# A fused attention and two-MLP kernel: the last 64 features of q and k in another matmul form, x loaded in two transfers, and another order of the program

## Chip, core and metric

One core of one Trainium2 chip runs the whole kernel. The metric is device time in microseconds (us), the median of several executions, lower is better. Engines are called as the profile does: PE (TensorE, matmuls), PEld (its weight loads, which overlap the matmuls), DVE (VectorE), ACT (ScalarE), POOL (GpSimd), SP (SyncE, whose queue issues the transfers).

## The reference

One sequence of 2048 tokens, 448 features, bf16. Attention has 16 heads of 28 features and a dilated local window: token s looks at the 8 tokens s, s-2, ..., s-14. Around it stand layer norms, a residual, and a block with two small MLPs. Cut to what matters:

```python
qkv = layernorm(x) @ wqkv                       # 2048 x 448 by 448 x 1344
logits[s, w] = q[s] . k[s - 2 w] / sqrt(28)     # w = 0..7, per head, -1e9 where s - 2 w < 0
o = sum over w of softmax(logits)[s, w] * v[s - 2 w]
h = x + o @ wo

b = layernorm(h)
g = gelu(layernorm(b) @ w1)                     # 448 x 448
g = four quarters of the features, shifted by +1, -1, +2, -2 tokens
x1 = b + g @ w2                                 # 448 x 448
h2 = gelu(layernorm(x1) @ w3) @ w4              # 448 x 1792, 1792 x 448
out = h + x1 + h2
```

## The kernel before

**Tiling.** Tokens go in 4 stages t of 512 (tiles of 128 tokens) through attention and w1, and then in 5 units u of 2, 4, 4, 4 and 2 tiles through w2, w3 and w4. The phases of a stage are N1 (layer norm of x), A1 (transpose the normalised tokens and project them on q and k), V (project on v), A2 (products of q with eight shifted copies of k on DVE, summed over a head's features by matmuls with a 0/1 matrix `zc`, then the softmax, which ends in `pb` and its transposed copy `pt`), A3 (`pt` spread by a mask into `bd_r` on DVE, then matmuls with the windowed values `vw`, then the product with wo, called O), B1 (two layer norms in one, a transpose, then w1 with gelu, called M). The phases of a unit are B2 (w2, residual), T (norm and transpose), W3 (w3, gelu) and B3 (w4, output). Stages and units overlap freely.

**Matmuls.** The contraction over 448 features lies in four chunks, whose upper and lower 64 partitions are separate matmuls, so that one with its weights in partitions 0 to 63 and one in 64 to 127 run side by side. `duo` (L459) makes two output tiles at once that way, in two operations: a first half (8 matmuls) and a second half (6), where tile and partition half change places. The second half carries an explicit wait for the end of the first (`op.sdeps.update(turned)`), because the two halves write the same two PSUM banks from opposite halves of the array. Other work may stand between the two.

**The last 64 features of q and of k** do not fill a block of 128 outputs. Before, A1 (L692 to L706) makes them as 64 x 64 quarters: four matmuls of 64 partitions by 64 outputs by 256 tokens form a set (two partition halves, two output halves), 28 matmuls a stage in two operations of 16 and 12, the second of which waits for the first in the same way. `X` is q, `Y` is k; the 512 tokens are split so that the even 64s of each 128 lie in the upper and the odd 64s in the lower 64 partitions of the output. ACT then evicts them: q as one 128 x 256 copy into `qT`, k as 128 x 4 x 64 into `kr`, which is four blocks of 80 columns (16 columns of earlier tokens ahead of 64 new ones), and the 16 earlier columns of each block in three small copies (L711 to L716).

**What sets the order of the work.** Every operation is recorded first, with its dependences. `ORDER` (L20) is a permutation of the operations' numbers, and each engine runs its own in that order; `OTHER` (L52) lists operations that go to their other engine (an eviction that is by default on ACT goes to DVE, a norm from ACT to DVE, one softmax product from DVE to POOL). All are emitted by one loop at L1010, so nearly every row of the profile has that line, and rows are told apart by names and shapes. SP issues all transfers in program order. `arrange` (L193) makes a DMA transpose wait for the landing of every transfer that stands ahead of it since the last such transpose, and later transfers wait for the transpose. Tokens of t = 0 and 1 are transposed by PE, those of t = 2 and 3 by a DMA transpose (`TURN`, first letters t and d).

**The start.** x is loaded as tile 0, tile 1 and tiles 2 and 3, then wqkv in two parts, then more x. `warm` (L647) puts 11 matmuls of 128 x 512 on a constant matrix ahead of everything on PE; `FILL` may put more of them behind the transposes of each of the first four tiles, and has none before. In A1 of t = 0 the matmuls go by pieces of 256 tokens.

## Time and profile before

| | |
|---|---|
| median of 3 runs | 188.77 us (188.72 to 190.16) |
| profiled execution, from first to last instruction | 186.4 us |
| PE busy, matmuls | 180.3 us, 97% of the span |
| PEld, DVE, ACT, POOL busy | 94.0, 127.0, 122.1, 24.0 us |
| bytes read from and written to memory | 8.14 and 1.84 MB |

The time of the profiled execution itself is given by its span alone: 186.4 us, which is 2.37 us below the median of the runs; that difference lies outside the first and last instruction. A busy share of 97% on PE says that little can be gained on other engines unless PE waits for them, and where it does has to be read by stages, since DVE and ACT are busy 68% and 65% of the whole span but not evenly.

A row of the timeline or of a group gives the start and the length in us, the engine, the line, the operation, out<-in by name, partitions x elements, the count, and in brackets how long the engine had idled and what ended that. On PE, "64*64" is partitions of the weights by outputs.

### The profile page before, as it was taken

What the parts mean: (1) busy time and instruction counts of PE and PEld (TensorE: products, weight loads), DVE (VectorE), ACT (ScalarE), POOL (GpSimd) and SP (SyncE); (2) the same over time, 40 slices, a digit from 0 to 9 for tenths busy, and PEclk for the clock granted to TensorE, in tenths of its full rate; (3) what the DMA queues carried; (4) which work ended last, traced back from release to release, by engine and by line L of the source; (5) the groups of instructions that cost most, each with busy time, mean ns of one, the idle gap of its engine ahead of it and who ended that gap; (6) DMA issues with size and microseconds to landing.
All of it is one profiled execution on the core that took longest, in us unless ns stands there. A gap on an engine that the chain in (4) does not pass through costs nothing.

```text
span 186.4 us, 5772 instructions
## 1 busy us (share of the span) xinstructions
PE 180.3 (97%) x2496; PEld 94.0 (50%) x2496; DVE 127.0 (68%) x225; ACT 122.1 (65%) x289; POOL 24.0 (13%) x59
## 2 busy tenths in 40 slices
PE   6899998999999999999999999999999999999994
PEld 2474333445544565765455544554445544555663
DVE  6799999999999999999476587614087274000403
ACT  3549999898999999957959489503833004730340
POOL 4320000000000000425300000170002805000000
PEclk9999999999999999999999999999999999999999
DMA  5999025865515667914360201491111602300121
GB/s 134 356 282 182 16 51 130 198 216 71 144 38 110 115 216 165 307 53 45 73 116 10 58 8 26 88 141 54 29 40 41 116 0 52 106 0 4 49 98 49
DMA packets 33633, 18.59 MB, mean 100 GB/s; under 512 B 21208, under 2 KB 33096, under 8 KB 33608
## 3 DMA queue, kind: packets, MB, share of 16 engines
q1 hardware_dynamic: 33608, 18.23, 41.5%
q8 instruction: 19, 0.31, 0.6%
q14 instruction: 6, 0.05, 0.1%
HBM read 8.14 MB, written 1.84 MB: 54 GB/s over the span
## 4 chain that ended last, share of the span: by engine, by line
PE 79%; DVE 14%; ACT 4%; DMA 1%; issue 0%; SPq 0%
PE ps L1010 79%; DVE qk_r L1010 9%; DVE st L1010 1%; ACT lntm L1010 1%; DMA xin<-in_A_x_dram 1%; DVE lntm L1010 1%; ACT L1010 1%; DVE mx L1010 1%; DVE xin L1010 1%; ACT arena L1010 1%; ACT h3T L1010 1%; DVE pb L1010 0%; DVE ls L1010 0%; DVE mv L1010 0%; ACT rs_x L1010 0%
## 5 line engine op out<-in xcount | busy, mean ns | idle before, releaser
L1010 PE MATMUL ps<-actT,arena 64*128 64x512 bf16 (+2 forms) x812 | 69.8, 326 | 0.9 <-DMA actT<-lntm 0.5
L1010 ACT ACTIVATE h3T<-ps 128x512 bf16<-128x512 f32 (+1 forms) x70 | 30.9, 517 | 38.5 <-PE ps L1010 38.4
L1010 PEld LDWEIGHTS ps<-actT,arena 64*128 64x128 bf16 (+1 forms) x812 | 35.4, 96 | 31.9 <-PE ps L1010 1.9
L1010 PE MATMUL ps<-arena,h3T 64*128 64x448 bf16 (+3 forms) x434 | 44.9, 343 | 0.2
L1010 ACT ACTIVATE arena<-ps 128x512 bf16<-128x512 f32 (+6 forms) x66 | 30.7, 508 | 8.5 <-PE ps L1010 8.1
L1010 PEld LDWEIGHTS ps<-arena,h3T 64*128 64x128 bf16 (+1 forms) x434 | 22.6, 94 | 20.0 <-ACT h3T L1010 0.6
L1010 DVE TENSOR_TENSOR qk_r<-arena 128x4096 bf16<-128x4096 bf16 (+1 forms) x16 | 31.9, 2013 | 0.1
L1010 DVE SCALAR_TENSOR_TENSOR qk_r<-ps,mrs,arena 128x448 bf16<-128x448 f32 (+2 forms) x17 | 10.4, 651 | 30.9 <-PE ps L1010 30.9
L1010 POOL TENSOR_TENSOR arena<-arena,xin 128x448 f32<-128x448 f32 x16 | 16.1, 1035 | 77.9 <-ACT lntm L1010 65.5
L1010 DVE TENSOR_TENSOR bd_r<-arena,bmask 80x2048 bf16<-80x2048 bf16 x16 | 19.0, 1214 | 1.7 <-PE ps L1010 1.7
L1010 DVE SCALAR_TENSOR_TENSOR arena<-xin,rs_y,ps 128x448 f32<-128x448 bf16 x16 | 10.3, 671 | 11.0 <-PE ps L1010 11.0
L1010 PE MATMUL ps<-wo_s,actT 64*128 64x448 bf16 x128 | 14.5, 350 | 0.1
L1010 PE MATMUL ps<-actT,w_s 64*112 64x512 bf16 x112 | 13.4, 379 | 0.0
L1010 PE MATMUL ps<-w_s,arena 64*128 64x448 bf16 x83 | 12.8, 349 | 0.1
L1010 PE MATMUL ps<-arena,actT 64*128 64x448 bf16 x112 | 12.3, 351 | 0.2
L1010 ACT ACTIVATE actT<-ps 128x512 bf16<-128x512 f32 (+2 forms) x19 | 11.7, 639 | 1.1 <-PE ps L1010 1.0
L1010 ACT ACTIVATE lntm<-xin,nm 128x448 bf16<-128x448 bf16 x16 | 10.6, 672 | 1.1 <-DVE nm L1010 1.1
L1010 DVE BATCH_NORM_STATS2 st<-xin 128x6 f32<-128x448 bf16 x16 | 9.2, 614 | 1.0 <-DMA xin<-in_A_x_dram 0.9
L1010 PEld LDWEIGHTS ps<-actT,w_s 64*112 64x112 bf16 x112 | 7.2, 126 | 4.4 <-ACT arena L1010 0.3
L1010 ACT ACTIVATE rs_x<-mv,epsilon 128x4 f32<-128x4 f32 (+2 forms) x16 | 4.6, 298 | 6.4 <-DVE mv L1010 6.3
L1010 PEld LDWEIGHTS ps<-w_s,arena 64*128 64x128 bf16 x83 | 5.5, 95 | 6.1 <-PE ps L1010 0.5
L1010 ACT ACTIVATE vt<-ps 128x448 bf16<-128x448 f32 x16 | 8.3, 546 | 0.5 <-PE ps L1010 0.5
(73 smaller groups left out, 161.6 us busy)
## 6 DMA issues: line engine op xcount, KB each, us to landing
arena<-in_B_w_dram SPq DMA_DIRECT2D x2, 896.0 KB, 5.9
out_dram<-qk_r SPq DMA_DIRECT2D x15, 112.0 KB, 1.8
arena<-in_B_w_dram SPq DMA_DIRECT2D x2, 784.0 KB, 7.3
vw<-vt SPq DMA_DIRECT2D x4, 320.0 KB, 4.3
vw<-vt SPq DMA_DIRECT2D x4, 256.0 KB, 4.1
arena<-in_A_wqkv_dram SPq DMA_DIRECT2D x2, 448.0 KB, 4.7
xin<-in_A_x_dram SPq DMA_DIRECT2D x2, 448.0 KB, 7.5
xin<-in_A_x_dram SPq DMA_DIRECT2D x3, 224.0 KB, 5.5
```

Of the source, the lines that this page charges most:

```text
L1010: inst = getattr(eng, meth)(**kw)
```

## The change

1. **The last 64 features of q and k become one block of 128 outputs.** POOL copies the 64 weight columns of q and the 64 of k side by side into a new tile `wl` (128 x 4 x 128), as the last operation of the setup (`setup_last`). A1 then makes a `duo` with `wl` as weights: `half(0)` is the first 256 tokens of the stage and `half(1)` the last 256, q in the upper and k in the lower 64 outputs; 8 and 6 matmuls of 64 partitions by 128 outputs by 256 tokens.
2. **Their evictions.** Each half gives two copies of 64 x 256 (q and k), and `kr` becomes one run of 16 + 256 columns with two small copies of 64 x 16 for the earlier tokens (one at t = 3). What lies in which partition half changes with it: now the halves are tokens 0 to 255 and 256 to 511, so the addressing in A2 (`lo`), in the turn of `pb`, in `pt` and in the mask product is permuted; shapes and counts stay the same there.
3. **The loads of x**: tile 0, then tiles 1 to 3 in one transfer, and the two parts of wqkv right behind.
4. **The start on PE**: `WARM` goes from 11 to 8, and `FILL` from none to one matmul each behind the transposes of tile 0 and of tile 1.
5. **A new `ORDER` and `OTHER`.** Of the operations that may go to either engine, those that change: two norms of B1 at t = 0 are on DVE instead of one; the softmax product of t = 3 goes from DVE to POOL; all four evictions of A3 at t = 3 are on DVE instead of three; the one of the first transposes that DVE evicted, and one norm of T at u = 0, go to ACT.

PE at the start. `ps<-ident 128x512` is a warm or fill matmul, `ps<-ident,lntm` a transpose, `ps<-actT,arena 64x256` the quarters and `ps<-actT,wl` the new form (the shape is that of the output). Before:

```order
L1010 MATMUL ps<-ident 128x512 x11
L1010 MATMUL ps<-ident,lntm 128x128 x16
L1010 MATMUL ps<-actT,arena 128x256 x66
L1010 MATMUL ps<-actT,arena 64x256 x16
L1010 MATMUL ps<-actT,arena 128x256 x6
L1010 MATMUL ps<-actT,arena 64x256 x12
```

PE at the start, with the change:

```order
L1007 MATMUL ps<-ident 128x512 x8
L1007 MATMUL ps<-ident,lntm 128x128 x4
L1007 MATMUL ps<-ident 128x512
L1007 MATMUL ps<-ident,lntm 128x128 x4
L1007 MATMUL ps<-ident 128x512
L1007 MATMUL ps<-ident,lntm 128x128 x8
L1007 MATMUL ps<-actT,arena 128x256 x64
L1007 MATMUL ps<-actT,wl 128x256 x8
L1007 MATMUL ps<-actT,arena 128x256 x8
L1007 MATMUL ps<-actT,wl 128x256 x6
```

Three warm matmuls are gone and two stand between the transposes; the 28 quarters are 14 matmuls, and in both orders something stands between their two operations at t = 0.

PE around the last group of t = 3 (`wo_s` is the product with wo, `qk_r,zc` the sums of A2, `arena,actT` the projection on v, `w_s` w1). Before:

```order
L1010 MATMUL ps<-qk_r,zc 32x32x8x2 x16
L1010 MATMUL ps<-arena,actT 128x448 x28
L1010 MATMUL ps<-qk_r,zc 32x32x8x2 x12
L1010 MATMUL ps<-actT,arena 128x512 x28
L1010 MATMUL ps<-actT,arena 64x256 x28
L1010 MATMUL ps<-actT,w_s 112x512 x28
```

With the change:

```order
L1007 MATMUL ps<-actT,wl 128x256 x8
L1007 MATMUL ps<-wo_s,actT 128x448 x8
L1007 MATMUL ps<-xin,ident 128x448 x2
L1007 MATMUL ps<-wo_s,actT 128x448 x8
L1007 MATMUL ps<-xin,ident 128x448 x2
L1007 MATMUL ps<-wo_s,actT 128x448 x8
L1007 MATMUL ps<-xin,ident 128x448 x2
L1007 MATMUL ps<-actT,wl 128x256 x6
L1007 MATMUL ps<-qk_r,zc 32x32x8x2 x24
```

The 28 quarters stood in one piece, so the second operation came directly behind the first; the new group's two halves have the products with wo between them. So they have at t = 0 and 2; at t = 1 the second half is directly behind the first.

SP around its first DMA transpose (`arena<-in_B_w_dram 128x2x1792` is half of w3; `vw<-vt` are the copies that build the windowed values). Before:

```order
L1010 DMA w_s<-in_B_w_dram 128x2x448 x2
L1010 DMA w_s<-in_B_w_dram 112x4x448
L1010 DMA_TRANSPOSE actT<-lntm 128x16x128
L1010 DMA vw<-vt 80x4x512
L1010 DMA vw<-vt 16x3x512
L1010 DMA vw<-vt 64x4x512
L1010 DMA vw<-vt 16x512
L1010 DMA vw<-vt 64x4x512
L1010 DMA vw<-vt 16x3x512
L1010 DMA vw<-vt 80x4x512
L1010 DMA arena<-in_B_w_dram 128x2x1792
```

With the change:

```order
L1007 DMA w_s<-in_B_w_dram 128x2x448 x2
L1007 DMA w_s<-in_B_w_dram 112x4x448
L1007 DMA arena<-in_B_w_dram 128x2x1792
L1007 DMA_TRANSPOSE actT<-lntm 128x16x128
L1007 DMA vw<-vt 80x4x512
L1007 DMA vw<-vt 64x4x512
L1007 DMA vw<-vt 16x3x512
L1007 DMA vw<-vt 64x4x512
L1007 DMA vw<-vt 16x3x512
L1007 DMA vw<-vt 16x512
L1007 DMA vw<-vt 80x4x512
```

The first half of w3 has moved from behind the seven copies to ahead of the transpose, which now waits for its landing.

The diff, cut to its core (of the two tables only the short one):

```diff
 OTHER = """
-92 182 483 489 492 495 546 552
+184 185 483 486 489 492 495 498 555
 """
-FILL = (0, 0, 0, 0)
-WARM = 11
+FILL = (1, 1, 0, 0)
+WARM = 8
...
+        wl = sb("wl", [128, 4, 128], BF16)
...
-        kr = [arv(A_KV + t * KVB + 3 * KVW, 128, 4 * KW).rearrange("p (j n) -> p j n", j=4) for t in range(NST)]
+        kr = [arv(A_KV + t * KVB + 3 * KVW, 128, PADK + 256) for t in range(NST)]
...
-        for i in range(2):
-            load_x(i, 1)
-        load_x(2, 2)
+        load_x(0, 1)
+        load_x(1, 3)
+        load_rows("wqk", wqkv_s[:, :, 0:2 * D], A_wqkv, 0, 2 * D)
         act(zs[:, 0, 0:1], epsilon[:, 0:1], ACT.Exp)
-        load_rows("wqk", wqkv_s[:, :, 0:2 * D], A_wqkv, 0, 2 * D)
...
+        def setup_last():
+            pool("tensor_copy", out=wl[:].rearrange("p c (g n) -> p c g n", g=2),
+                 in_=wqkv_s[:, :, D - 64:3 * D - 64].rearrange("p c (g n) -> p c g n", g=2)[:, :, :, 0:64])
...
-            X, Y = _Tile(P_bank), _Tile(P_bank)
-            both = ((X, D - 64, ((0, 1, 2, 3), (0, 2, 3))), (Y, 2 * D - 64, ((0, 1, 3), (0, 1, 2, 3))))
...
-            copy(qT[:, 3, now:now + 256], X(lambda v: v[:, 0:256]))
-            copy(kr[t][:, :, PADK:], Y(lambda v: v[:, 0:256].rearrange("p (j n) -> p j n", j=4)), False)
-            copy(kr[t][64:128, :, 0:PADK], last(0, 0, 4), False)
-            copy(kr[t][0:64, 1:4, 0:PADK], last(0, 1, 3), False)
+            ends = []
+
+            def half(h):
+                b = _Tile(P_bank)
+                ends.append(b)
+                return sums(lambda lo, n: b(lambda v: v[:, 0:256].rearrange("p (i n) -> p i n", i=2)),
+                            lambda c, part: wl[part, c, :],
+                            lambda c, part, lo, n: rows(a, c, 2 * h, 2, part), h == 0)
+
+            duo(half(0), half(1), ((0, 256),))
+            for h, b in enumerate(ends):
+                copy(qT[64 * h:64 * h + 64, 3, now:now + 256], b(lambda v: v[0:64, 0:256]))
+                copy(kr[t][64 * h:64 * h + 64, PADK:], b(lambda v: v[64:128, 0:256]), False)
+            copy(kr[t][64:128, 0:PADK], ends[0](lambda v: v[64:128, 256 - PADK:256]), False)
             if t + 1 < NST:
-                copy(kr[t + 1][0:64, 0:1, 0:PADK], last(3, 1, 1), False)
+                copy(kr[t + 1][0:64, 0:PADK], ends[1](lambda v: v[64:128, 256 - PADK:256]), False)
...
-                        lo = (2 * j + e if c < 3 else j) * 512
+                        lo = (4 * e + j) * 512
...
         setup()
+        setup_last()
```

35 lines of the change are left out of this document (10 added, 25 removed), and 61 rows, old and new, of the table ORDER.

## The prediction

> **What bounds the kernel now.** I read the page first: the share of each engine, and the chain of work that ended last.
>
> ```profile
> span 186.4 us, 5772 instructions
> PE 180.3 (97%) x2496; PEld 94.0 (50%) x2496; DVE 127.0 (68%) x225; ACT 122.1 (65%) x289; POOL 24.0 (13%) x59
> PE 79%; DVE 14%; ACT 4%; DMA 1%; issue 0%; SPq 0%
> ```
>
> PE works nearly all the time and carries 79% of the chain, so fewer or shorter matmuls should show. But 14% of the chain is DVE, so the next view is the busy time by stretches (columns: stretch, its length, then busy us of PE, PEld, DVE, ACT, POOL, granted clock, DMA share, GB/s).
>
> ```profile
> 14.30:35.00 20.70, 19.83 (x249) 8.03 (x246) 20.70 (x24) 20.03 (x55) 0.00 (x0) 1.00 0.51 103
> 35.00:62.00 27.00, 26.79 (x548) 12.73 (x552) 26.95 (x39) 25.84 (x69) 0.00 (x0) 1.00 0.53 119
> 62.00:80.00 18.00, 17.95 (x334) 11.01 (x328) 17.86 (x24) 17.65 (x40) 2.03 (x2) 1.00 0.81 217
> 88.70:108.00 19.30, 19.23 (x314) 10.03 (x311) 11.60 (x20) 14.26 (x32) 1.45 (x3) 1.00 0.29 61
> ```
>
> From 14.3 to 80 us PE, DVE and ACT are all full: of 65.70 us DVE is idle 0.19 and ACT 0.67 + 1.16 + 0.35 = 2.18. PE is idle 0.87 of the first 20.7 us and hardly after. Only behind 88.7 us do DVE and ACT have air. A shorter matmul is worth its time only if PE finds other work earlier, and in the full stretch any earlier work that needs DVE or ACT finds them taken.
>
> **The change part by part.** First the group of the last 64 features: the weight loads of the quarters at t = 3 (first three rows) and at t = 0 (next four), and two PE rows with matmuls of the new form's shape, 64 x 128 by 256 columns, and what follows them.
>
> ```profile
> 61.06 0.36 PEld L1010 LDWEIGHTS ps<-actT,arena 64*64 64x64 bf16 x16 [0.42 <-issue]
> 61.77 0.25 PEld L1010 LDWEIGHTS ps<-actT,arena 64*64 64x64 bf16 x12 [0.34 <-PE ps L1010]
> 62.22 0.82 PEld L1010 LDWEIGHTS ps<-actT,w_s 64*112 64x112 bf16 x10 [0.20 <-ACT mx L1010]
> ...
> 12.05 0.36 PEld L1010 LDWEIGHTS ps<-actT,arena 64*64 64x64 bf16 x16 [0.21 <-issue]
> 12.61 0.22 PEld L1010 LDWEIGHTS ps<-actT,arena 64*128 64x128 bf16 x6 [0.20 <-issue]
> 13.04 0.25 PEld L1010 LDWEIGHTS ps<-actT,arena 64*64 64x64 bf16 x12 [0.21 <-issue]
> 13.50 0.22 PEld L1010 LDWEIGHTS ps<-actT,arena 64*128 64x128 bf16 x6 [0.20 <-issue]
> ...
> 76.64 4.00 PE L1010 MATMUL ps<-actT,arena 64*128 64x256 bf16 x70
> 80.47 0.92 PE L1010 MATMUL ps<-wo_s,actT 64*128 64x448 bf16 x8
> ```
>
> Start to start, the quarters of t = 3 take 62.22 - 61.06 = 1.16 us, with their second operation held for the end of the first. At t = 0, where another group stands between, they take (12.61 - 12.05) + (13.50 - 13.04) = 1.02. The new form: 80.47 - 76.64 = 3.83 us for 70, 55 ns each, so 14 take 0.77. That saves 0.25 at t = 0 and 0.39 at each other t, together **1.42 us**. A second half directly behind its first costs between 0.14 (1.16 against 1.02) and 0.34 (the idle of the weight loads); I take 0.23.
>
> The trace shows how many there are:
>
> ```profile
> PEld ps L1010 <- PE ps L1010: 4.4, 10, 0.6
> ```
>
> Ten such waits of PEld until 104.5 us, three of them in the quarters and so in the 1.42. The new order has seven second halves directly behind their firsts, one of them the new group's at t = 1: outside the quarters seven before and seven after, so nothing more. The rows of t = 0 also show 0.2 us of idle where the form changes; the new program changes between tiling by rows and by columns once more, and part of that is in the starts used above: **+0.15** (0 to 0.2). PE as a whole: -1.27, with bounds -0.9 (one such wait more than I count, at 0.34, and the change of form at 0.2) and -1.42.
>
> A rule of the Trainium skill speaks against this term. Row: 28 quarters 1.02 us unhindered, 14 halves 0.77. Rule (TensorE: Matmul & The Clock Gate, Part 3: Packing small matmuls): tiles of the array that run together span one matmul plus about 4 ns for each further tile. By it seven sets of four would take an estimated 7 x (107 + 12) ns = 0.83 us, 0.06 above 14 halves, and the term would be 0.25 plus three waits of 0.23, about 0.9 in all. The trace disagrees (1.02), and I keep 1.42.
>
> **The evictions.** The columns are ACT's groups between 8.1 and 80 us: busy, mean ns.
>
> ```profile
> L1010 ACT ACTIVATE arena<-ps 128x256 bf16<-128x256 f32 x8 | 2.9, 392 | 0.0
> L1010 ACT ACTIVATE arena<-ps 64x64 bf16<-64x64 f32 x4 | 0.9, 216 | 0.1
> L1010 ACT ACTIVATE arena<-ps 64x48 bf16<-64x48 f32 x4 | 0.8, 208 | 0.1
> L1010 ACT ACTIVATE arena<-ps 64x16 bf16<-64x16 f32 x3 | 0.5, 181 | 0.1
> L1010 ACT ACTIVATE lntm<-xin,nmr,rs_y 128x512 bf16<-128x512 bf16 x3 | 2.2, 819 | 0.0
> L1010 ACT ACTIVATE lntm<-arena,nmr,rs_y 128x448 bf16<-128x448 f32 x1 | 0.8, 750 | 0.0
> ```
>
> Before, a stage costs ACT 392 x 2 + 216 + 208 + 181 = 1.39 us. A 64 x 256 copy has not been seen; by elements per partition it is nearest to 128 x 256 (392; below it 216 for 64 columns). After: 4 x 392 + 2 x 181 = 1.93, so +0.54 a stage, +2.16 over four (bounds: 4 x 216 + 362 = 1.23, so -0.6, to +2.16). A norm of B1 leaves ACT (-0.82), one of T comes (+0.75). Net **+2.1 us on ACT** in the very stretch where it has 2.18 us idle, part of which is idle because PE was late:
>
> ```profile
> ACT arena L1010 <- PE ps L1010: 1.0, 3, 0.4
> ACT vt L1010 <- PE ps L1010: 0.5, 1, 0.5
> ```
>
> So ACT becomes as full as DVE, and PE can't be fed faster than these two allow. This is what I hold against the full 1.27.
>
> **The start.**
>
> ```profile
> 0.81 1.35 SPq L1010 DMA_DIRECT2D xin<-in_A_x_dram  x3
> 2.20 0.98 SPq L1010 DMA_DIRECT2D arena<-in_A_wqkv_dram  x2
> 1.63 4.61 PE L1010 MATMUL ps<-ident 128*128 128x512 bf16 x11 [1.63 <-POOL mhalf L1010]
> 6.30 0.62 PE L1010 MATMUL ps<-ident,lntm 128*128 128x128 bf16 x8
> L1010 PE MATMUL ps<-ident,lntm 128*128 128x128 bf16 x16 | 1.3, 221 | 0.5 <-DVE lntm L1010 0.5
> 8.10 0.36 PEld L1010 LDWEIGHTS ps<-actT,arena 64*128 64x128 bf16 x8 [0.18 <-ACT actT L1010]
> 8.71 0.63 DVE L1010 BATCH_NORM_STATS2 st<-xin 128x6 f32<-128x448 bf16 x1 [0.46 <-DMA xin<-in_A_x_dram]
> 14.28 2.29 DVE L1010 TENSOR_TENSOR qk_r<-arena 128x4096 bf16<-128x4096 bf16 x1
> ```
>
> An issue takes SP 1.35 / 3 = 0.45 us. One issue fewer lets wqkv and the x of t = 1 leave up to 0.45 earlier; tile 1 comes later, as it now shares a transfer with tiles 2 and 3. DVE's work for t = 1 waits for that x at 8.71, and from there it runs on into the full stretch that begins at 14.28. So DVE, and with it the rest, can move forward by 0 to 0.45 us; I take **-0.35**. The warm matmuls end ahead of the transposes in either version and the two fills stand where PE waits for norms (cover: 6.30 to 8.10); if that cover were gone they would cost 2 x 0.42.
>
> `wl` needs a POOL copy of 128 x 512, bounded by these:
>
> ```profile
> L1010 POOL MEMSET vw<- 16x512 bf16 x1 | 0.5, 515 | 0.0
> L1010 POOL TENSOR_TENSOR arena<-arena,xin 128x448 f32<-128x448 f32 x16 | 16.1, 1035 | 77.9 <-ACT lntm L1010 65.5 <-DVE lntm L1010 12.4
> ```
>
> 0.5 to 1.0 us from when wqkv has landed, ahead of the first matmuls at 8.10, and needed at about 11.5: nothing. Behind it on POOL wait the late fills for A2, whose first product starts at 14.28: covered too. The softmax product on POOL at t = 3 (about 1.0 by the same row) lies where DVE has air.
>
> **w3 ahead of the transpose.**
>
> ```profile
> 25.53 2.09 SPq L1010 DMA_TRANSPOSE actT<-lntm  x1
> 35.58 0.61 SPq L1010 DMA_DIRECT2D arena<-in_B_w_dram  x1
> 29.97 3.19 PE L1010 MATMUL ps<-actT,arena 64*128 64x512 bf16 x28 [0.49 <-DMA actT<-lntm]
> DMA  0279999999999999300000019901988998983006
> GB/s 0 84 176 257 357 349 343 356 366 377 291 148 229 182 224 178 65 26 0 7 7 0 0 27 213 214 12 41 238 184 182 175 247 195 293 314 124 3 0 107
> ```
>
> The last two rows are the DMA share and rate from 0 to 45 us in 40 slices: nearly idle from about 19 to 25.5 us, a hole of six slices. 896 KB at the 350 GB/s of the slices behind the start is an estimated 2.6 us, so it lands ahead of 25.5 and holds nothing up; if it landed later, the first matmuls of A1 at t = 2 would come later by as much. The wait of 0.49 us for that transpose stays, as DVE's chain sets its time. The vw copies gain nothing PE waits for.
>
> **The sum.** Against the profiled 186.4: PE -1.27 and the start -0.35 is -1.6 if all counts. If DVE and ACT give nothing back, only the start counts: -0.35. The truth lies between; PE can pull forward products with v, wo and w3, each with evictions on ACT, which has no room for all. I take two thirds, **-1.0**: span 185.4, plus the 2.37 us between the profiled span and the median of the runs, **187.8 us**.
>
> **The rivals.**
>
> *All of it counts, and some stalls go as well.* For it: PE's waits are short, and products are indeed put between the halves at t = 2 and 3. Against: the full DVE. -1.6, with the 0.49 for the transpose -2.1: 186.7 to 187.2, and 186.3 with what I left out.
>
> *ACT becomes the bound.* Place: the evictions of A1 and V at t = 1 to 3. Price: +2.1 us of ACT, of which only idle that PE did not cause can take a part, 2.18 - 1.5 = 0.7; +1.4 less the start's 0.35 is +1.05, so 189.8. It decides once a 64 x 256 copy costs over about 300 ns (4 x 300 + 362 - 1390 = +0.17 us a stage, 0.7 over four). Against: ACT's waits for PE vanish too when PE is early; half of it gives 189.2.
>
> *The clock opens later.* The warm matmuls ran at 0.42 us each, eight transposes of a quarter of the columns behind them took 0.62 with the length of the last one (221 ns in the groups by form); (0.62 - 0.22) / 7 = 0.057 each against 0.42 / 4 = 0.105: half speed until about 6 us. With 8 they end at about 5.0, and then come gaps. If the half speed lasted two to five us longer, A1 at t = 0, which runs from 8.10 to about 14, would lose 1 to 2.5: 188.8 to 190.3. For: three matmuls fewer; against: transposes and fills follow them, and the granted clock is 1.00 in every stretch above. The Trainium skill (TensorE: Matmul & The Clock Gate, Part 1: The HAM clock gate) says that PE starts throttled and that a free-running window of about 3.4 us of activity releases it; activity from 1.63 would do so between about 5.0 and 8.5 us. The trace agrees with the early part.
>
> *Nothing comes through.* x and the fetches are hidden (no wait in this trace is ended by an instruction fetch), the DVE chain sets the stage: 188.4 to 188.8.
>
> **How the numbers follow.** Forecast (187.3 to 188.3) 0.42; all counts 0.27; ACT bound 0.15; clock 0.06; nothing 0.10. A measurement tells about 1%, 1.9 us, from no change. Faster by that needs under 186.88: most of the second case and a trace of the first, 0.24. Slower by it needs over 190.66: tails of two cases, 0.07. Within: 0.69. The range reaches down through all of "all counts" and up to the middle of "ACT bound": 186.3 to 189.5.
>
> **What would show it.** Right: the group 64*128 by 256 has 56 matmuls more at about 55 ns, PE busy falls by 1 to 1.5 us, DVE stays full from about 14 to 80, ACT's busy time there rises by about 2. The first qk_r product begins at about 13.9. Wrong: PE idle in waits for `arena` or `vt` evictions on ACT (the ACT rival); first A1 matmuls over 0.1 us apart (clock); a wait for the transpose over 1 us (w3 came late); the wl group held by POOL.

## The result, and the profile after

| | before | with the change |
|---|---|---|
| median of 4 runs, same chip | 189.17 us (188.72 to 190.16) | 196.49 us (195.46 to 198.27) |
| ratio, 95% interval | | 1.0391 [1.0326, 1.0456] |
| span of the profiled execution | 186.4 us | 195.4 us |

The change makes the kernel about 3.9% slower. The forecast was 187.8 us, and the time is 7 us above the upper end of the range: it was wrong in sign. In all executions here the time is 1.7 to 1.9 us above the span (197.17 against 195.4), so only that much of the 2.37 us lies outside the first and last instruction; the rest is that the profiled execution before was shorter than the median one. The forecast does not move by it.

Executions over 1.5% above the fastest of the same kernel, most of them at a lower granted clock of PE, are left out of all ratios and medians, which leaves two of kernel 2 below, and the profiles of kernels 2 and 16, taken of such executions, are not read.

From the page of the changed kernel: the busy times and the two rows of the chain that ended last.

```profile
span 195.4 us, 5673 instructions
PE 181.7 (93%) x2439; PEld 99.3 (51%) x2439; DVE 128.2 (66%) x224; ACT 128.9 (66%) x295; POOL 26.8 (14%) x61
PE 46%; DMA 17%; DVE 16%; ACT 16%; issue 1%; POOL 1%; SPq 1%
PE ps L1007 46%; DMA actT<-lntm 13%; ACT arena L1007 7%; DVE lntm L1007 5%; DVE st L1007 4%; ACT lntm L1007 3%; ACT vt L1007 3%; DVE arena L1007 2%; DMA out_dram<-qk_r 2%; DVE qk_r L1007 2%; DMA xin<-in_A_x_dram 2%; ACT actT L1007 1%; DVE bd_r L1007 1%; POOL rs_y L1007 1%; ACT xin L1007 1%
```

PE's busy time is hardly changed, 181.7 against 180.3 us, but the span is 9 us longer: the time went into waits of PE. The chain is the plainest sign: PE's share of it fell from 79% to 46%, and DMA's rose from 1% to 17%, 13% of it in `actT<-lntm`, which is the DMA transpose of normalised tokens.

The busy time by stretches, in the columns that the prediction explained:

```profile
14.30:35.00 20.70, 18.55 (x222) 7.80 (x213) 18.65 (x22) 19.95 (x53) 0.00 (x0) 1.00 0.52 124
35.00:62.00 27.00, 24.57 (x514) 11.83 (x516) 24.94 (x34) 24.62 (x65) 0.00 (x0) 1.00 0.37 93
62.00:80.00 18.00, 17.60 (x250) 9.56 (x246) 17.40 (x23) 17.62 (x42) 0.24 (x2) 1.00 0.80 167
```

DVE, which was full from 14.3 to 80 us (0.19 us idle), is idle 4.71 us there now, and PE 4.98 instead of 1.13. ACT is idle 3.51 us there, so it is not full either. No engine became the bound: the engines now wait for each other and for the transposes. The waits of PE's matmuls, summed by what ended them (us, times, longest), show for whom most:

```profile
PE ps L1007 <- DMA actT<-lntm: 5.7, 6, 1.6
```

Before there was one such wait, of 0.5 us. With the smaller ones for other engines PE's waits behind its first matmul come to 9.0 us in this view, against 1.0 before. Four of the six for transposes, with the transposes that end them (SP rows: the issue and its length; where a row has two transposes, it is the first):

```profile
51.91 0.93 PE L1007 MATMUL ps<-arena,actT 64*128 64x448 bf16 x8 [1.58 <-DMA actT<-lntm]
97.35 7.08 PE L1007 MATMUL ps<-actT,arena 64*128 64x512 bf16 x64 [1.25 <-DMA actT<-lntm]
127.00 3.23 PE L1007 MATMUL ps<-actT,w_s 64*112 64x512 bf16 x28 [1.20 <-DMA actT<-lntm]
155.13 1.04 PE L1007 MATMUL ps<-actT,arena 64*128 64x512 bf16 x8 [1.09 <-DMA actT<-lntm]
```
```profile
45.85 1.98 SPq L1007 DMA_TRANSPOSE actT<-lntm  x1
91.90 9.66 SPq L1007 DMA_TRANSPOSE actT<-lntm  x2
121.43 7.33 SPq L1007 DMA_TRANSPOSE actT<-lntm  x2
150.72 1.95 SPq L1007 DMA_TRANSPOSE actT<-lntm  x1
```

The uses of the same last three transposes in the kernel before, with no wait in brackets:

```profile
85.73 8.99 SPq L1010 DMA_TRANSPOSE actT<-lntm  x2
114.71 7.50 SPq L1010 DMA_TRANSPOSE actT<-lntm  x2
144.42 1.96 SPq L1010 DMA_TRANSPOSE actT<-lntm  x1
```
```profile
91.06 4.36 PE L1010 MATMUL ps<-actT,arena 64*128 64x512 bf16 x38
121.03 1.89 PE L1010 MATMUL ps<-actT,w_s 64*112 64x512 bf16 x16
151.85 1.46 PE L1010 MATMUL ps<-actT,arena 64*128 64x512 bf16 x12
```

Read together these give the **cover**: how long after the issue PE comes to the matmul that needs the transpose. Before: 91.06 - 85.73 = 5.33, 6.32 and 7.43 us. After, less the wait: 97.35 - 1.25 - 91.90 = 4.20, 4.37 and 3.32 us. A transpose lands 5.4 us after its issue in the first two of these (below). The new order leaves them less of PE's other work.

Why 5.4 us? The next view is the DMA share of the window from 121.0 to 126.9 us of the changed kernel in 40 slices, its queues, and the time from issue to landing (us, last number):

```profile
q8 instruction: 1, 0.02, 1.6%
...
actT<-lntm SPq DMA_TRANSPOSE x1, 5.4
```

and of the window of the same transpose before, from 114 to 120 us:

```profile
DMA  0000000000000899999999999999950000000100
...
actT<-lntm SPq DMA_TRANSPOSE x1, 4.3
```

A slice of the DMA row after, with a window of the same length (121 to 127), shows what differs:

```profile
DMA  0000000000679999600000000199999999900000
```

Before, the 2080 packets run in one piece and the transpose takes 4.3 us. After, there is a hole of some 2 us in it, and one packet of 16 KB on queue q8, which is a fetch of instructions (19 of them in the program, 0.31 MB). That they are PE's is inferred: they come earlier when PE gets 30 or 33 matmuls more at its start (kernels 9, 15 and 17). I had read in the waits that none is ended by an instruction fetch, and concluded that fetches are hidden. They are, until one falls into the flight of a transpose. In the trace of before, the transposes of four tiles take 4.3 to 4.4 us without a q8 packet in their flight, and with one between 4.3 and 5.2; after, 4.3 to 4.4 without, and 4.8, 5.4, 5.4 and 6.0 with one.

### The profile page after: what moved, and what is told of

Read it like the earlier page. It is cut to its first block, busy times and chain, and to the rows that moved or that the text cites. A ratio compares the mean times of both kernels' runs of the same rounds, so it can differ in the third digit from the quotient of the medians.

```text
span 195.4 us, 5673 instructions
## 1 busy us (share of the span) xinstructions
PE 181.7 (93%) x2439; PEld 99.3 (51%) x2439; DVE 128.2 (66%) x224; ACT 128.9 (66%) x295; POOL 26.8 (14%) x61
## 4 chain that ended last, share of the span: by engine, by line
PE 46%; DMA 17%; DVE 16%; ACT 16%; issue 1%; POOL 1%; SPq 1%
PE ps L1007 46%; DMA actT<-lntm 13%; ACT arena L1007 7%; DVE lntm L1007 5%; DVE st L1007 4%; ACT lntm L1007 3%; ACT vt L1007 3%; DVE arena L1007 2%; DMA out_dram<-qk_r 2%; DVE qk_r L1007 2%; DMA xin<-in_A_x_dram 2%; ACT actT L1007 1%; DVE bd_r L1007 1%; POOL rs_y L1007 1%; ACT xin L1007 1%
## 5 line engine op out<-in xcount | busy, mean ns | idle before, releaser
L1007 PE MATMUL ps<-actT,arena 64*128 64x512 bf16 (+1 forms) x700 | 67.4, 337 | 3.0 <-DMA actT<-lntm 2.6
L1007 PEld LDWEIGHTS ps<-actT,arena 64*128 64x128 bf16 x700 | 34.5, 95 | 29.5 <-DMA actT<-lntm 3.2
L1007 ACT ACTIVATE arena<-ps 128x512 bf16<-128x512 f32 (+4 forms) x70 | 32.4, 506 | 6.6 <-PE ps L1007 5.8
L1007 PEld LDWEIGHTS ps<-arena,h3T 64*128 64x128 bf16 (+1 forms) x434 | 24.1, 94 | 18.4 <-issue 0.2
L1007 PE MATMUL ps<-arena,actT 64*128 64x448 bf16 x112 | 13.0, 351 | 1.8 <-DMA actT<-lntm 1.6
L1007 POOL TENSOR_TENSOR mrs<-nm,rs_y 128x4 f32<-128x4 f32 x4 | 1.7, 425 | 76.5 <-ACT rs_y L1007 65.8
L1007 PEld LDWEIGHTS ps<-actT,w_s 64*112 64x112 bf16 x112 | 8.1, 127 | 5.8 <-DVE lntm L1007 1.6
L1007 DVE TENSOR_SCALAR lntm<-arena,mv,rs_y 128x512 bf16<-128x512 f32 x14 | 8.2, 642 | 3.7 <-POOL rs_y L1007 3.1
```

What stands on the lines that cost most here:

```text
L1007: inst = getattr(eng, meth)(**kw)
```

## The experiments

Ratios are to the kernel before on the same chip, with the 95% interval. The kernel before itself takes between 189.4 and 190.2 us on these chips, so kernels are compared by their ratios, and the difference of two ratios is less sure than either.

**Theory after seeing the result.** The late order lacks cover, and fetches lengthen transposes. **Rivals:** the new form with its longer work on ACT; the later start; the early order. The first four kernels divide the change. Where a kernel has its own numbering, `ORDER` and `OTHER` are the same operations renumbered.

**1. The new form alone**, in the order, with the loads and the warm matmuls of before.

```diff
-load_x(0, 1); load_x(1, 3); load_rows("wqk", ...)
+load_x(0, 1); load_x(1, 1); load_x(2, 2); ...; load_rows("wqk", ...)
-FILL = (1, 1, 0, 0); WARM = 8; ORDER and OTHER of the change
+FILL = (0, 0, 0, 0); WARM = 11; ORDER and OTHER of before
```

> The kernel before with the new matmul form of the last 64 features and its evictions alone; loads, warm matmuls and order as before (the new operations stand where the old ones stood; one eviction of pt stands 3 places earlier since the new layout needs it). Theory A, the loss is in the new order, in which evictions and transposes stand too late: 187.0 to 189.0, with ACT about 2 us busier and PE about 1.3 us less busy than before. Theory B, the loss is in the form, whose five evictions a stage overload ACT: 192 to 196, with DVE waits for evictions of ACT of over 1 us before 35 us.

192.16 us, 1.0122 [1.0056, 1.0189]. Half as many matmuls for the group, in the same order, make the kernel slower by more than a percent.

**2. The old form in all the rest of the change.**

```diff
-duo(half(0), half(1), ((0, 256),)) and its copies
+the quarters X, Y and their copies, as before
```

> The changed kernel with the old quarters and their evictions put back at the places of the new ones; loads, warm matmuls and order stay as changed. Theory A (order): 194 to 197, about as slow as the changed kernel. Theory B (form): 187.5 to 190.

192.01 and 192.65 us, 1.0115 [1.0033, 1.0197], from two executions only. So the rest alone is not the whole loss, nor is the form alone.

**3. The whole change in the order of before** (form, loads, fills).

```diff
-ORDER, OTHER of the change
+ORDER, OTHER of before
```

> The changed kernel in the order and with the engine choices of before; form, loads, warm and fill matmuls as changed. Theory A (order): 187.5 to 189.5. Theory B (form): 192 to 196. A third, that the loads of x and the start cost the time: over 190 here while the form alone stays under 189.

194.22 us, 1.0223 [1.0163, 1.0284]. The order is worth about 1.7% of the 3.9%, with 0.9% either way by the two intervals.

**4. One eviction earlier.** DVE's wait of 2.05 us, up to 23.93, for the last copy of q at t = 0 was the longest early stall of the change; here that copy stands nine places earlier on ACT.

```diff
-... six evictions and norms ..., copy(qT, half 1 of t = 0)
+copy(qT, half 1 of t = 0), ... six evictions and norms ...
```

> The changed kernel with one eviction moved: the copy of q's second half at t = 0 stands on ACT behind k's second half, nine places earlier than in the changed order. If DVE's wait of 2.05 us at 21.9 us is the root of the delay: it vanishes and the time falls by 1.5 to 2.5, to 194 to 195. If the delay is given by ACT's total work in that stretch: the same wait turns up behind another eviction and the time stays at 196 to 197.

196.53 us, 1.0336 [1.0279, 1.0393]. The interval overlaps that of the change. DVE's wait for that copy is gone, and right behind that product it waits 1.73 us for a norm step of ACT. PE's wait of 0.73 us at 24.6 for DVE's product is gone and one of 0.41 stands at 29.8; its waits for an eviction (0.52 at 34.8) and for the transpose (1.50 at 50.5) stand as in the change. So this one stall of DVE was not what mattered.

**5. The evictions alone.** The kernel before with its quarters, and each of the two large copies a stage split in two halves of 64 partitions. The matmuls stay.

```diff
-copy(qT[:, 3, ...], X(...)); copy(kr[t][:, :, PADK:], Y(...))
+for p in (TOP, BOT): copy(qT[p, 3, ...], X(...))
+for p in (TOP, BOT): copy(kr[t][p, :, PADK:], Y(...))
```

> The kernel before, in its own order, with the quarters as they are, but their two large evictions a stage (q and k) each made as two copies of 64 partitions, as many as the new form needs: +0.7 us of ACT a stage, +2.7 in all, and nothing else changed. If the form alone was slower because of its ACT work: ratio to before 1.008 to 1.016 (1.5 to 3 us), with PE waiting for arena and vt evictions near 18 and 31 us as in the form alone. If it was slower because of the new matmuls' places or the permuted layout: 0.997 to 1.004.

192.34 us, 1.0123 [1.0078, 1.0168]: as much as the whole new form. PE's waits in this kernel, two of its five over half a us:

```profile
19.57 2.33 PE L1019 MATMUL ps<-actT,arena 64*128 64x512 bf16 x20 [0.64 <-ACT arena L1019]
32.75 2.33 PE L1019 MATMUL ps<-actT,arena 64*128 64x512 bf16 x20 [1.09 <-ACT vt L1019]
```

and in the kernel with the form alone:

```profile
19.13 2.33 PE L1014 MATMUL ps<-actT,arena 64*128 64x512 bf16 x20 [0.57 <-ACT arena L1014]
32.05 2.33 PE L1014 MATMUL ps<-actT,arena 64*128 64x512 bf16 x20 [0.83 <-ACT vt L1014]
```

The same two waits in the same places: PE waits for banks that ACT has not yet emptied. Neither stood in the kernel before. ACT is busy 125.7 us in kernel 5 and 125.1 in kernel 1, against 122.1 before.

**6 and 7. The loads and the fills**, each alone in the kernel before.

```diff
-load_x(0, 1); load_x(1, 1); load_x(2, 2)
+load_x(0, 1); load_x(1, 3)
```
```diff
-FILL = (0, 0, 0, 0); WARM = 11
+FILL = (1, 1, 0, 0); WARM = 8
```

> The kernel before with x loaded as tile 0 and tiles 1 to 3 and nothing else changed. The old order with all other changes was about 2 us slower than the form alone, and its first evictions 1.3 us later. If the shared transfer is the cause: ratio 1.005 to 1.012, with A1's first matmuls and first qk_r product 0.5 to 1.3 us later. If not: 0.997 to 1.003.

> The kernel before with 8 warm matmuls instead of 11 and one fill matmul each behind the transposes of the first two tiles, nothing else changed. If the fills or a slower clock are the cause of the late start: ratio 1.005 to 1.012, with transposes of tiles 2 and 3 later or matmuls of A1 further apart than 55 ns. If not: 0.997 to 1.003.

190.29 us, 1.0031 [0.9996, 1.0067], and 190.39 us, 1.0028 [0.9997, 1.0058]. Neither can be told from no change, and the loads bring no gain that shows. Kernel 3 against kernel 1 gives about 1.0% for both together. There is a place where the two work together. The stretch from 9 to 10 us of the kernel before, and of the change:

```profile
9.00:10.00 1.00, 1.00 (x24) 0.88 (x21) 1.00 (x3) 0.00 (x0) 0.95 (x8) 1.00 1.10 366
```
```profile
9.00:10.00 1.00, 1.00 (x14) 0.70 (x10) 1.00 (x3) 0.84 (x2) 0.97 (x8) 1.00 1.09 380
```

PE is busy all of it in both, and gets through 24 matmuls in the one and 14 in the other. Pairs of matmuls of 256 columns start 0.11 us apart before, and 0.21 us apart in the change until 10.1 us: half speed, while the column of the granted clock says 1.00. So it is in the profiled executions of the change and of kernels 3, 4 and 9; in kernels 6 and 7, with the loads or the fills alone, it is not. Nor is it in that of kernel 8, which has both.

**8. Early order, late order.** The change with its order up to the last A2 sum of t = 3, at about 80 us, and the order of before from there.

```diff
-ORDER, OTHER = first part and second part of the change
+ORDER, OTHER = first part of the change, second part of before
```

> The changed program, in the changed order up to the last sum of A2 at t = 3 (about 80 us), and from there all remaining operations in the order of before. If the changed order of the second part lacks cover behind its DMA transposes (the waits of 1.1 to 1.4 us at 96, 126 and 154 us): these waits go and the time falls by 2 to 4, to 192.5 to 194.5. If they come only from the delay of the first part: they stay, 196 to 197.

193.93 us, 1.0216 [1.0161, 1.0271], as kernel 3. The late order costs about 1.7%, with 0.9% either way, and no late wait for a transpose is left. What the early order costs is not told by this: kernels 3 and 8 agree to within 0.8%, but the profiled execution of kernel 8, which was at full speed from 7.0 us, took 193.81 us, and that of kernel 3, at half speed until about 10.4, 193.83.

**9. The fetches moved.** The change, each warm and fill matmul of 512 columns made as four of 128: the same columns, and 30 more matmuls, so PE's fetches come some 60 instructions earlier in its program.

```diff
-return mm(busy(), ident[:], ... 512 columns)
+return mms([(busy(... 128 * j ...), ident[:], ident[:], ...) for j in range(4)], after)
```

> The changed kernel with each of its 10 warm and fill matmuls of 512 columns made as four of 128: the same columns, 30 matmuls with their weight loads more, so that every later instruction fetch of PE falls 60 instructions earlier in the program. In the changed kernel's trace four of the critical DMA transposes had an instruction fetch in their flight and took 4.8 to 6.0 us, the others 4.3 to 4.4. Counted along its PE instructions the shift leaves only the one at 45.9 us with a fetch. If fetches lengthen the transposes: those issued near 61, 91.9 and 121.4 us land after 4.3 to 4.4 us, PE's waits at 96 and 126 us fall below 0.4, ratio to before 1.020 to 1.030 (1.039 unshifted). If the long transposes have another cause: 1.033 to 1.045 and they stay long.

195.00 us, 1.0274 [1.0237, 1.0312], 1.2% less than the change (0.4 to 1.9 by the two intervals), with the same work. The transpose near 46 us takes 4.9 us instead of 6.0, and PE waits 0.42 for it instead of 1.58. Those at 90.95 and 120.39 land after 4.4 and 4.3 us; the wait of PE for the first is 0.35 instead of 1.25,

```profile
95.35 7.08 PE L1007 MATMUL ps<-actT,arena 64*128 64x512 bf16 x64 [0.35 <-DMA actT<-lntm]
```

and for the second none instead of 1.20. The third, which no fetch had met and which has the least cover, keeps its wait: 1.08 after 1.09. A fetch now meets the transpose at 98.67, which takes 5.9 us where it took 4.3, and PE waits 0.88 for it.

**10. The late order alone**, in the kernel before.

```diff
-ORDER, OTHER = first part and second part of before
+ORDER, OTHER = first part of before, second part of the change
```

> The kernel before in its own order up to the last sum of A2 at t = 3, and from there all remaining operations in the changed order; form, loads and warm as before. In the changed program the changed second part cost about 1.7% more than the old one. If that order has too little work behind its DMA transposes whatever comes before: ratio 1.008 to 1.018, with PE waits for transposes of about 1 us. If it is slow only behind a first part that is late: 0.997 to 1.005.

192.50 us, 1.0157 [1.0116, 1.0197]. Two of its waits:

```profile
126.97 1.25 PE L1017 MATMUL ps<-actT,arena 64*128 64x512 bf16 x10 [0.97 <-DMA actT<-lntm]
149.91 1.04 PE L1017 MATMUL ps<-actT,arena 64*128 64x512 bf16 x8 [1.07 <-DMA actT<-lntm]
```

The transpose that ends the first took 5.9 us, the one that ends the second 4.3. So the late order waits even where no fetch is in the way: the cover is short by itself, and a fetch adds to it.

**11 and 12. Small copies on POOL**, to take work from ACT: the short copies of earlier columns of k, in the kernel before and in kernel 1.

```diff
-copy(kr[t][64:128, :, 0:PADK], last(0, 0, 4), False)
+pool_copy(kr[t][64:128, :, 0:PADK], kr[t][0:64, :, 64:])
... (the others likewise; each waits for its neighbours on POOL)
```

> The kernel before with work taken off ACT: the small copies of earlier k columns (three a stage for the last 64 features and one for the rest) are made by POOL from the evicted k instead of by ACT, 216 + 208 + 181 + 245 ns a stage, about 3 us in all in the stretch where POOL is idle. ACT as the bound: ratio 0.985 to 0.996, PE's and DVE's waits for ACT in the first 80 us shrink. DVE as the bound, which is as full: 0.997 to 1.003. If POOL disturbs DVE or comes late for the qk_r products: 1.004 or more.

> The new form alone, order, loads and warm as before, with the small copies of earlier k columns on POOL in the same way. The form alone was at 1.012. If only the ACT work of its evictions made it slower, it now has about as much ACT work as the kernel before and its shorter PE work shows: 0.990 to 1.002, PE's waits for arena and vt evictions gone. If something else in the form is slow: 1.006 to 1.013.

191.41 us, 1.0101 [1.0068, 1.0134], and 192.33 us, 1.0156 [1.0112, 1.0201]. Nothing is told by these about ACT, since POOL became late: in kernel 11 ACT waits 1.49 us for it, up to 56.15. A group of POOL's copies there (busy, mean ns):

```profile
L1026 POOL COPY arena<-arena 64x16 bf16<-64x16 bf16 x3 | 10.7, 3578 | 6.4 <-ACT arena L1026 6.3
```

**13 and 14. Less work on ACT** by leaving out most of the sums of x at t = 3, in the kernel before and in kernel 1.

```diff
-act(normalized(ln, at + n), src(i), ACT.Square, ...)
+act(ln(... one column ...), src(i)[:, 0:1], ACT.Square, ...)
... (the sum of x likewise)
```

> The kernel before with ACT work left out: the mean and the square sum of x at t = 3 (8 ACT passes of 448 columns between 19 and 33 us) are taken over one column instead of 448, so the norm of t = 3 has wrong statistics; about 3 us less on ACT in the full stretch, order as before. If ACT sets the pace there: ratio 0.985 to 0.995. If DVE or PE do: 0.997 to 1.003. With a later fetch in the transpose issued near 43 us: up to 0.004 more.

> The new form alone with the same ACT work left out (mean and square sum of x at t = 3 over one column). If the form was at 1.012 because of its 2 to 3 us more on ACT: now 0.990 to 1.001, and PE's waits for arena and vt evictions near 18 and 31 us are gone. If instruction fetches or the permuted layout made it slow: 1.006 to 1.013, with those waits gone all the same.

189.45 us, 0.9985 [0.9955, 1.0014], and 190.94 us, 1.0067 [1.0039, 1.0095]. Leaving them out takes 2.3 us from ACT in kernel 13 and 2.8 in kernel 14. Before, that brings nothing. With the new form the ratio falls from 1.0122 to 1.0067, but these two intervals overlap; kernels 17 and 18 below, the same pair on one chip with moved fetches, differ by 1.1 us (0.4 to 1.8), which is clear of noise. So with the form about 0.5% of the time goes with this work of ACT at t = 3. The wait for `vt` at 31.2 is gone, the one at 18.5 stays at 0.58, and it too is for ACT; whether ACT's copies make all of the loss is not shown.

**15. The fetches moved in the kernel before** (as kernel 9, 33 matmuls more).

```diff
-return mm(busy(), ident[:], ... 512 columns)
+return mms([(busy(... 128 * j ...), ident[:], ident[:], ...) for j in range(4)], after)
```

> The kernel before with each warm matmul of 512 columns made as four of 128: nothing else changes, but every instruction fetch of PE comes 66 instructions earlier in the program. Counted along the PE instructions of the trace of before, the fetch at 44.3 us, one us into its transpose, is replaced by one near 46, three us into it. If fetches that come late in a transpose hold it and PE: that transpose takes 5.8 to 6.0 us instead of 4.65, PE has a wait of 0.5 to 1.0 us near 44 to 50 in the mask matmuls, ratio 1.002 to 1.006. If fetches cost nothing here: 0.998 to 1.002.

190.86 us, 1.0046 [1.0013, 1.0079]: half a percent from the place of the fetches alone. The ratio is as expected and the place is not: the transpose near 44 takes 5.2 us, not 5.8 to 6.0, and PE stops for 0.30 us in its flight. Two others got long instead, the first (5.5) and the one issued at 62.94 (5.4), for which PE waits 1.04 us. The first transpose, and what PE waits for it (0.49 us before):

```profile
actT<-lntm SPq DMA_TRANSPOSE x1, 5.5
```
```profile
31.08 3.20 PE L1010 MATMUL ps<-actT,arena 64*128 64x512 bf16 x28 [1.40 <-DMA actT<-lntm]
```

Its issue is at 25.53 as before, to the hundredth. It lands 1.1 us later, with one q8 packet in its window, and PE waits 0.91 us longer.

**16. Only the first half of w3 ahead of the first transpose**, in the kernel before.

```diff
-DMA_TRANSPOSE actT, seven vw copies, DMA arena<-in_B_w_dram
+DMA arena<-in_B_w_dram, DMA_TRANSPOSE actT, seven vw copies
```

> The kernel before with the first half of w3 loaded ahead of the first DMA transpose, as in the change, and nothing else. By the hole in the DMA row it costs nothing: 0.998 to 1.002, the first transpose is issued as early as before. If it held the transpose: 1.003 or more and the wait of A1 at t = 2 grows beyond 0.5 us. If the vw copies profit: below 0.998.

189.53 us, 0.9966 [0.9938, 0.9994]. It costs nothing, as predicted, and is the only one of these kernels that beats the one before, by a third of a percent. That is just below the range expected for "costs nothing", on the side named for the vw copies; whether they are the reason is not shown.

**17 and 18. The fetches moved in the kernel with the form alone**, and in the same with less work on ACT. Kernels 1 and 14 had transposes of 5.5 to 6.1 us and two waits that I put down to them, so this was to bring back half of the loss, or all but a little.

> The new form alone, with each warm matmul of 512 columns made as four of 128, so that PE's instruction fetches come 66 instructions earlier. The form alone was at 1.012; its transpose near 59 us took 5.5 us with a fetch 2.7 us into it and PE then waited 0.2 and 0.8 us. Counted along its PE instructions the shift leaves a fetch only in the transposes near 45 (as before), and within 0.6 to 1.2 us of the start of those near 89 and 118. If fetches are half of the form's cost: the transpose near 59 takes 4.3, the waits behind it fall below 0.4, ratio 1.004 to 1.009. If ACT's evictions are all of it: 1.010 to 1.014.

> The same shift in the form with the ACT passes of t = 3 left out (mean and square sum over one column, as in the form with light ACT, which was at 1.007). If ACT's evictions and the fetches together make up the form's cost: 0.996 to 1.003. If a third cause is left: 1.005 or more.

193.05 us, 1.0135 [1.0087, 1.0183], and 191.76 us, 1.0088 [1.0053, 1.0123]: no gain. My theory of fetches fell here, for the form, though the transposes did get short (in kernel 17 4.6, 4.3 and 4.4 us where kernel 1 has 5.9, 5.5 and 6.1; a fourth, near 90 us, got longer, 4.8 instead of 4.3). What became of the wait of kernel 1 at 68 us (first row) in kernel 17 (second fence):

```profile
68.89 1.47 PE L1014 MATMUL ps<-actT,w_s 64*112 64x512 bf16 x11 [0.83 <-DMA actT<-lntm]
```
```profile
69.25 1.07 PE L1014 MATMUL ps<-actT,w_s 64*112 64x512 bf16 x8 [1.08 <-ACT arena L1014]
```

The wait is still there and has another owner. ACT at this place in kernel 17, and before:

```profile
65.40 1.40 ACT L1014 ACTIVATE arena<-ps 64x256 bf16<-64x256 f32 x3
66.82 1.28 ACT L1014 ACT_TABLE_LOAD   x1
68.11 2.06 ACT L1014 ACTIVATE arena<-ps 112x512 bf16<-112x512 f32 x4
```
```profile
62.69 0.89 ACT L1010 ACTIVATE arena<-ps 128x256 bf16<-128x256 f32 x2
63.60 1.28 ACT L1010 ACT_TABLE_LOAD   x1
64.90 6.08 ACT L1010 ACTIVATE arena<-ps 112x512 bf16<-112x512 f32 x13
```

The copies of the form at t = 3 stand ahead of the table load for gelu, and w1's gelus behind it. There 1.40 us of copies stand where 0.89 stood, and PE's next products with w1 need the banks that those gelus empty. The transpose and the gelus were late by about as much, and taking away one leaves the other. That reading comes from the rows; the copies behind the gelus were not tried.

## Why the prediction was wrong, point by point

**The step that failed** is first of all the one that costs the order: the sum has a term for the form, one for the evictions and one for the start, and none for the new place of matmuls around the transposes in the second half. The order appears in it only as a gain, "PE can pull forward products with v, wo and w3". The text took its floor from "If DVE and ACT give nothing back, only the start counts", and weighed PE's waits in the stretch up to 80 us, since DVE and ACT have air behind it. It should have asked of each transpose how much of PE's work lies between its issue and its use. The sign "a wait for the transpose over 1 us" came four times, and not because w3 came late (kernel 16). Kernel 10 puts the late order alone at +1.6%, 3 us, and kernels 8 and 3 say about the same of the change, +1.7%. The second step that failed is the sign of the form's term: about -0.85 us in the forecast (two thirds of 1.27), +1.2% or 2.3 us alone in kernel 1.

**Fetches are hidden (the argument in the last rival): false.** Queue q8 was in the page of before, with 19 packets, and the transposes of before differ among themselves (4.3 to 5.2 us), and only those with a q8 packet in their flight are over 4.5. Moving the fetches changes the time by 1.2% in the change (kernel 9), by 0.5% the other way in the kernel before (kernel 15), and by nothing that can be told in the form alone (kernel 17). The Trainium skill (Runtime: NRT & Kernel Launch, Instruction fetch mechanics) says that engines fetch in blocks of 16 KiB and that crossing a boundary is "mostly hidden". The trace agrees with the size; where a transpose is in flight it doesn't agree with the rest: 5.4 instead of 4.3 us.

**The term of the form.** Its PE part has the right size: at t = 0 its two operations take 13.35 - 12.91 and 14.11 - 13.78, together 0.77 us as predicted,

```profile
12.91 0.60 PE L1007 MATMUL ps<-actT,wl 64*128 64x256 bf16 x8
13.35 0.60 PE L1007 MATMUL ps<-actT,arena 64*128 64x256 bf16 x8
13.78 0.49 PE L1007 MATMUL ps<-actT,wl 64*128 64x256 bf16 x6
14.11 0.63 PE L1007 MATMUL ps<-ident,lntm 64*128 64x64 bf16 x32
```

and ACT's part too: 376 ns for a 64 x 256 copy where I took 392,

```profile
L1007 ACT ACTIVATE arena<-ps 64x256 bf16<-64x256 f32 x16 | 6.0, 376 | 0.3
```

What was wrong is the share of it that reaches the time. I took two thirds of PE's 1.27 us and of the start's 0.35 as gain. PE's busy time, which was to fall by 1 to 1.5 us, is 0.4 us higher in kernel 1 than before and 1.4 higher with the change. Kernel 5 shows that the split of the evictions alone costs 1.2%, as much as the whole form in kernel 1. A gain from the shorter matmuls does not show; one as small as the predicted 1.27 us, 0.7%, could hide in the two intervals. The prediction had said that DVE and ACT allow no more, and then counted most of it all the same.

**The rival "ACT becomes the bound"** had the sign and the place, at t = 1 to 3, but not the mechanism. ACT isn't full after the change, and taking 2.3 us from it in the kernel before brings nothing (kernel 13). It is the time at which single copies come: PE waits 0.57 and 0.83 us at 18.5 and 31.2 for banks, and 2.8 us less on ACT take away the second of these and about 0.5% (kernels 14 and 18). That the times of single copies make the rest is argued, not shown. I had set ACT's price by adding up busy time, 189.2 to 189.8, at most 1.4 us for the evictions; the form alone costs 2.3.

**The start** was to bring -0.35 us and brought no gain that shows. In the changed kernel A1's matmuls begin at 8.65, before at 8.13, ACT's first evictions at 12.46, before at 11.67; and the first product of DVE, which I predicted at 13.9, at 14.38.

```profile
8.65 4.42 PE L1007 MATMUL ps<-actT,arena 64*128 64x256 bf16 x64
12.46 2.48 ACT L1007 ACTIVATE arena<-ps 128x512 bf16<-128x512 f32 x5 [0.93 <-PE ps L1007]
14.38 2.27 DVE L1007 TENSOR_TENSOR qk_r<-arena 128x4096 bf16<-128x4096 bf16 x1
```

In the kernel before, the loads and the fills alone measure 0.3% each, which can't be told from nothing (kernels 6 and 7). With the form and the order of before, both together cost 1.0% (kernel 3 against kernel 1), and the traces say where: the first matmul of A1 starts 0.6 us later, and from 11 us on all of kernel 3 runs 1.3 us behind kernel 1. The other 0.7 us come while it is at half speed.

**The rival "the clock opens later"**, which I gave 0.06, came true in the profiled execution: A1's first matmuls are 0.1 us apart each, 0.21 a pair, until 10.1 us, the sign that I had named. In these traces it appears only where loads and fills are both changed, but the program alone does not decide it. Kernel 8 runs the same matmuls in the same order up to the last A2 sum of t = 3; there PE stands still for 0.74 us ahead of the transposes of tile 1, where the change has 0.59, and yet it is at full speed from 7.0 us. So these two traces give its price. The last A2 sum of t = 3, with the change and in kernel 8:

```profile
80.37 0.40 PE L1007 MATMUL ps<-qk_r,zc 128*32 128x512 bf16 x4
79.77 0.40 PE L1013 MATMUL ps<-qk_r,zc 128*32 128x512 bf16 x4
```

The change is 0.96 us behind kernel 8 near 12 us, 0.55 from 20 to 50 us, and 0.60 here. I had set the price at 1.0 to 2.5 us; it is about 0.6 of the 9.0 us, by one execution of each. With the Trainium skill's window of about 3.4 us (TensorE: Matmul & The Clock Gate, Part 1: The HAM clock gate) I had estimated full speed by about 8.5 us. The trace of the change, with 10.1, doesn't agree, and that of kernel 8, with 7.0, does.

**What was right.** w3 ahead of the transpose costs nothing (kernel 16), and the group of `wl` isn't held by POOL. The wait of 0.49 us "for that transpose stays" is nearly right, 0.31, but the transpose itself is issued 1.6 us later than before.

**What stays open.** The parts, each alone in the kernel before, are 1.2% (form), 0.3% and 0.3% (loads, fills, neither told from nothing) and 1.6% (late order), 3.4% of 3.9%; but the change without the form loses only 1.2% (kernel 2, two executions) and not 2.7%, so they do not simply add. The profiled executions place the two large parts. The last A2 sum of t = 3 starts at 76.21 us before; kernel 1 is 3.4 us late there and 3.6 at the end, kernel 10 is not late there and 3.3 at the end, and the change is 4.2 us late there and 9.0 at the end. Behind this mark the change loses 4.8 us, and kernel 8, with the late order of before, 2.1. So the form's loss is made ahead of the mark, and the late order's behind it. Of the form's 1.2%, about 0.5% goes with ACT's work at t = 3 (kernels 17 and 18); of the rest, the wait at 68 us is read from rows and wasn't tried by an experiment. What the early order costs stays open too: in kernel 8 it ends with kernel 3, which had lost some 0.7 us to half speed.

## What to carry to other kernels

For each DMA transpose, or other transfer that PE will need, work out how much of PE's work stands between its issue and its use, before and after the change, and hold it against its longest time, not its usual one: 4.3 us alone, up to 6 with a fetch in its flight. A change in the number of matmuls ahead of it moves the fetches of the whole program behind it, and with them the time: down by 1.2% in one kernel here, up by 0.5% in another, not at all in a third. So two programs that differ a little should be compared by their transposes first. And where a wait may have two late releasers, taking away one can show nothing, as in kernel 17: look at who owns the wait next.

## What the runs showed of the hardware that was not expected

- A DMA transpose of four tiles takes 4.3 to 4.4 us from issue to landing. In the traces of these kernels, every one over 4.6 us has a 16 KB instruction fetch (queue q8) in its flight, but not every fetch does harm: with one 0.5 to 1.3 us behind the issue they took 4.6 to 5.4 us, 2 to 3 us behind it 5.1 to 5.7, and 3.4 to 4.3 us behind it anything from 4.3 (two in the kernel before) to 6.1 (kernel 1). What decides the last is open.
- PE can run at half speed with a granted clock of 1.00 in the same row of the profile: 14 matmuls against 24 in the stretch from 9 to 10 us. The starts of the matmuls show it, the column doesn't. Of two kernels with the same matmuls up to there, one (kernel 8) had left it by 7.0 us and the other (the change) at 10.1.
- With a fetch in the flight of a transpose PE can stop in the middle of one group of matmuls, waiting for nothing that the profile names ("issue"): in kernel 1 0.66 us between matmul 45 and 46 of the 64 mask products, until 0.18 us after the transpose issued at 44.82 landed. That it waits there for its own instructions is a reading, not shown.

```profile
49.72 0.53 PE L1014 MATMUL ps<-bd_r,vw 80*32 80x64 bf16 x45
50.91 0.33 PE L1014 MATMUL ps<-bd_r,vw 80*32 80x64 bf16 x19 [0.66 <-issue]
```

- A POOL copy can last as long as DVE's long products beside it: in kernel 12 one of 64 x 16 bf16 took 8.8 us, from 47.42 to 56.24, while DVE ran products until 56.19, and others of 64 x 16 took 0.19 us at 17.73 and 29.19, beside a norm step and a maximum on DVE.
- A copy by ACT costs by its columns and not by its partitions: 376 ns for 64 x 256, where 128 x 256 took 392. So splitting a copy by partitions nearly doubles its time on ACT.
